# A linear-attention and FFN kernel: another planned order of the first tile, and batch 0's key sums from a product with a column of ones

## The chip, the cores and the metric

The kernel runs on one core of one Trainium2 chip. The metric is the device time of one execution in microseconds (us), the median of several. The engines are TensorE (PE; weight loads are a row of their own, PEld), VectorE (DVE), ScalarE (ACT) and GpSimd (POOL). SyncE (SP) only issues DMAs here.

## The reference

q, k and v have 8 batches, 8 heads, a sequence of 576 and a head size of 64. The attention is linear: no product of queries with keys, but a 64 by 64 matrix for each head.

```python
q_s = exp(q - max(q, axis=d));   q_s /= sum(q_s, axis=d) + 1e-9
k_s = exp(k - max(k, axis=seq)); k_s /= sum(k_s, axis=seq) + 1e-9
kv  = einsum('bhsd,bhse->bhde', k_s, v)
x   = einsum('bhsd,bhde->bhse', q_s, kv)      # -> 4608 tokens x 512
h   = maximum(x @ w_in, 0)                    # 512 -> 2048
out = (h * h) @ w_out                         # 2048 -> 512
```

The two weight matrices arrive in double precision; q, k and v in single.

## The kernel before

**Tiles.** The work is done in nine tiles of 512 tokens. Tiles 0 to 7 are the first 512 positions of each batch; the last 64 positions of all batches (their x goes to the DRAM tensor `x_tail`) make the ninth. A batch's eight heads are handled as four pairs p of two heads (128 channels). The hidden size is cut into 16 steps f of 128.

**The FFN of a tile.** For each f, the first product `h_f` is 12 matmuls of 512 columns: for each of the four pairs high half of x times high half of w_in, low half of x times high half, high half of x times low half (`xh`, `xl`; x is split into two rounded parts so that the sum is close to single precision). After relu and square, split again, the second product adds into four accumulators `acc_0` to `acc_3` (128 tokens each), three matmuls each.

**Weights.** The 16 "words" u (`load_words`, L478) are the weights as 64-bit numbers, 1 MB each in two halves of 512 KB: word 0 has the w_in blocks of f = 0 and 1, word u the w_in block of f = u + 1 and the w_out block of f = u − 1, the last two what is left. ACT scales both 32-bit parts of a word (`scale_words`: two rows `raw` of 1024), DVE and POOL join them (`join_words`), ACT casts the high half (row `w`) and POOL subtracts for the low half. Words 0 to 11 have their own buffers. Words 12 to 15 lie in a pool `late`, which can only be opened when every tile of the pool `boot` (batch 0's attention) has been used for the last time.

**Batch 0 ("boot").** The first tile needs batch 0's x, so this attention runs ahead of any FFN work. For each pair: k is transposed (`kT`, PE), DVE takes the maximum along the sequence, ACT does exp (`first_exp`, L826) with the sum along the row taken as the engine goes (`accum_out`, an extra ACCUMULATOR read), exp of the tail's 64 positions likewise, POOL adds both sums, DVE takes the reciprocal (`ks2`); PE transposes back (`ek`, `ekt`), `kv_product` (L905) multiplies with v (8 matmuls of 64 columns and 2 for the tail), `kv_split` (L949) scales by `ks2` on its way out of PSUM. `x_product` (L978) multiplies with the transposed q (`qT`) in two halves of 288 columns; ACT copies the high part, DVE subtracts for the low part, ACT copies the tail's 64 columns to `xt`. A single-precision matmul shows as two records.

**Batch 1 and later.** Batch 1's attention is interleaved with the FFN of tile 0. Its k stays untransposed: DVE reduces k, then a second step takes in the k tail (`kt`), a small step `sm` follows, PE transposes the maximum (`kmT`) and the rest follows; the denominators there come from a column of ones beside v, so that `ps[:, D]` of the kv product has the sum (`kv_scale`, L939, which for batch 0 returns at once).

**What sets the order.** Everything recorded for tile 0 (all such rows show line L100) goes through `Planner` (L126). Each instruction, or group under `together`, is a node with a cost; `order` (L256) walks through time, takes the earliest node that can start and, among those on its engine within `WAIT`, the one with the greatest priority (`tail`); a load ends at the running DMA time plus `moved / RATE` plus `LAND`. `shift` moves the priorities of some nodes for each number in `SEEDS`. The result is the program order of every engine, SP included. `fill` (L1511) puts transposes that nobody reads (`idle`, L1514) into PE's planned gaps before the first h. After tile 0's attention work everything has a fixed order.

Of the kernel before, what the change touches and what calls it, by code (L numbers as in the profile page):

```python
# [15 lines left out]
AF = mybir.ActivationFunctionType  # L16
ALU = mybir.AluOpType
# [97 lines left out]
class Node:  # L115


    def __init__(self, engine):
# [4 lines left out]
        self.since = 0.0  # L123


class Planner:  # L126
# [5 lines left out]
    ISSUE, LAND, RATE = 0.65, 2.2, 350.0  # L132
    READY, COLD, FILL, SPARE = 1.0, 0.25, 0.14, 0.2
    WAIT = 0.25

# [7 lines left out]
    def together(self, chained=False):  # L143
# [6 lines left out]
        node, self.into = self.into, None  # L150
        if chained:
            if self.chain is not None:
                node.before[self.chain] = True
            self.chain = node
# [101 lines left out]
    def order(self):  # L256
# [7 lines left out]
        free, dma, told = {}, 0.0, []  # L264
        self.banks = {}
        while ready:
# [20 lines left out]
            )  # L287
            n.start, n.end = t, t + n.busy
# [48 lines left out]
def attention_ffn(  # L337
# [26 lines left out]
    B, H, SQ, D = q.shape  # L364
    DM = H * D
    DF = w_in.shape[1]
    P = 128
# [13 lines left out]
    STEP = 0.0  # L381
    SEEDS = (
# [556 lines left out]
    def kv_scale(b, p):  # L939

        if b == 0:
            return
# [1256 lines left out]
```

## Time and profile before

| | |
|---|---|
| median of 3 runs | 829.72 us (829.48 to 831.48) |
| the profiled execution | 830.97 us |
| its span in the trace | 829.0 us |
| mean granted TensorE clock | 0.999 |

A profile row names an engine, a line, an operation and its tile with what it reads, then partitions by elements. Buffer numbers are left out in the trace's answers, so `h` is `h_f` of any step. "[0.81 <-ACT xh]" behind a row is the time that the engine stood idle ahead of it, and what released it. In the chain of waits each line is a start, a length and what the end of the program hung on there. For DMA issues the columns are count, size of each, and the time from issue to landing.

### The profile page before, as it was taken

Reading aid. Unit: us, or ns where it says so; the run is one execution under the profiler, and the core shown is the slowest. Engines: PE = TensorE matmul, PEld = TensorE weight load, DVE = VectorE, ACT = ScalarE, POOL = GpSimd, SP = SyncE. Lnnn points to the kernel's source line nnn. Section 1 sums busy time; section 2 is a strip of 40 time slices with the busy share of each in tenths; the row PEclk is TensorE's granted clock in tenths of the full one; section 3 lists DMA queues with packets and bytes.
Section 4 is the critical chain, followed back from the end, with each engine's and each line's share of the span. In section 5 each row is a group of like instructions: output and inputs, shape, how many; then the busy total and the mean of one; then the engine's idle time right before and its main releaser. Section 6 shows DMA issues by size and latency. Waiting matters only on the chain.

```text
span 829.0 us, 12870 instructions
## 1 busy us (share of the span) xinstructions
PE 816.2 (98%) x4411; PEld 662.5 (80%) x4411; DVE 620.5 (75%) x1134; ACT 481.7 (58%) x882; POOL 143.9 (17%) x151
## 2 busy tenths in 40 slices
PE   8999999999999999999999999999999999999997
PEld 7677777788888888788888787888888888888886
DVE  6888876877668656878667675577888987866995
ACT  6988844665655555655565566455754545665442
POOL 5889990001001001001001000000310000000000
PEclk9999999999999999999999999999999999999999
DMA  9993114435535446355446452766776778579455
GB/s 274 379 342 129 39 28 135 124 111 147 120 115 125 128 160 173 99 170 119 117 134 148 151 141 96 235 225 212 261 283 196 226 229 238 181 237 385 136 173 98
DMA packets 219297, 145.48 MB, mean 175 GB/s; under 512 B 146528, under 2 KB 193120, under 8 KB 219232
## 3 DMA queue, kind: packets, MB, share of 16 engines
q1 hardware_dynamic: 213312, 142.96, 56.9%
q10 hardware_dynamic: 5920, 1.71, 0.9%
q8 instruction: 35, 0.57, 0.3%
q14 instruction: 30, 0.25, 0.1%
HBM read 97.52 MB, written 46.66 MB: 174 GB/s over the span
## 4 chain that ended last, share of the span: by engine, by line
PE 84%; DMA 5%; SPq 4%; DVE 4%; ACT 2%; issue 1%; POOL 0%; DVEq 0%; ACTq 0%
PE acc L100 22%; PE h L100 20%; PE out L1865 18%; PE h L1308 17%; SPq L100 4%; PE h_kv L100 2%; PE x L100 2%; DMA k<-in_k_dram 1%; DMA qn<-in_k_dram 1%; DMA raw<-in_moe_w_out_dram 1%; DMA ring<-w_sums 1%; DVE bst L100 1%; ACT r L100 1%; DVE km L100 0%; DMA kt<-in_k_dram 0%
## 5 line engine op out<-in xcount | busy, mean ns | idle before, releaser
L100 PE MATMUL h<-xh,w 128*128 128x512 f32 x632 | 208.8, 392 | 1.0 <-ACT xh L100 0.8
L100 PE MATMUL acc<-w,gh 128*128 128x512 f32 x632 | 197.2, 393 | 0.0
L1865 PE MATMUL out<-w,w 128*128 128x512 f32 x636 | 148.9, 389 | 0.0
L100 PEld LDWEIGHTS h<-xh,w 128*128 128x128 f32 x632 | 118.6, 188 | 27.9 <-ACT xh L100 1.3
L1865 PEld LDWEIGHTS out<-w,w 128*128 128x128 f32 x636 | 119.3, 188 | 25.1 <-DVE w L100 0.2
L100 PEld LDWEIGHTS acc<-w,gh 128*128 128x128 f32 x632 | 117.0, 188 | 26.3 <-issue 1.7
L100 PE MATMUL acc<-w,gl 128*128 128x512 f32 x316 | 123.1, 390 | 0.0
L100 PE MATMUL h<-xl,w 128*128 128x512 f32 x316 | 123.1, 389 | 0.0
L100 DVE TENSOR_TENSOR gl<-r,gh 128x512 fp32r<-128x512 f32 x64 | 44.1, 688 | 73.2 <-ACT gh L100 72.6
L100 ACT ACTIVATE r<-h 128x512 f32<-128x512 f32 x79 | 47.1, 596 | 85.2 <-PE h L100 85.0
L100 POOL PARTITION_ALL_REDUCE kmx<-km x24 | 26.7, 1111 | 337.2 <-DVE km L100 337.2
L100 PEld LDWEIGHTS h<-xl,w 128*128 128x128 f32 x316 | 59.4, 188 | 12.5 <-DVE xl L100 0.4
L100 PEld LDWEIGHTS acc<-w,gl 128*128 128x128 f32 x316 | 59.3, 188 | 12.4
L1308 PE MATMUL h<-w,w 128*128 128x512 f32 x288 | 69.2, 389 | 0.0
L100 ACT COPY u<-h 128x512 f32<-128x512 f32 x48 | 28.0, 583 | 62.8 <-PE h L1308 62.7
L1308 PEld LDWEIGHTS h<-w,w 128*128 128x128 f32 x288 | 54.1, 188 | 11.2
L100 ACT CAST gh<-r 128x512 fp32r<-128x512 f32 x64 | 39.5, 617 | 21.5 <-PE acc L100 21.0
L100 ACT CAST w<-w 128x1024 fp32r<-128x1024 f32 (+1 forms) x38 | 38.0, 1006 | 18.4 <-PE out L1865 8.7
L1308 PE MATMUL h<-w,ring 128*128 128x512 f32 x192 | 46.4, 390 | 0.2 <-DMA ring<-w_sums 0.2
L100 DVE TENSOR_TENSOR c<-h,u 128x512 f32<-128x512 f32 x48 | 33.0, 687 | 13.6 <-ACT u L100 7.0
L1308 PEld LDWEIGHTS h<-w,ring 128*128 128x128 f32 x192 | 35.9, 188 | 8.1 <-PE h L1308 0.6
L100 POOL TENSOR_TENSOR w<-w,raw 128x512 int32<-128x512 int32 x32 | 41.8, 1327 | 1.7 <-DVE w L100 1.1
(236 smaller groups left out, 1290.1 us busy)
## 6 DMA issues: line engine op xcount, KB each, us to landing
w<-wo_sums SPq DMA_DIRECT2D x64, 256.0 KB, 3.4
g_b<-c SPq DMA_DIRECT2D x60, 256.0 KB, 2.6
w<-g_b SPq DMA_DIRECT2D x18, 512.0 KB, 7.8
raw<-in_moe_w_in_dram SPq DMA_DIRECT2D x16, 512.0 KB, 7.9
raw<-in_moe_w_out_dram SPq DMA_DIRECT2D x16, 512.0 KB, 8.5
v<-in_v_dram SPq DMA_DIRECT2D x56, 128.0 KB, 3.0
q<-in_q_dram SPq DMA_DIRECT2D x96, 72.0 KB, 2.3
k<-in_k_dram SPq DMA_DIRECT2D x20, 256.0 KB, 4.1
```

The lines of the kernel that those rows point to most:

```text
L100: getattr(self.eng, op)(*map(real, args), **{k: real(a) for k, a in kwargs.items()})
L1308: nc.tensor.matmul(out=out.real(), lhsT=a[:, k * P:(k + 1) * P].real(), rhs=m[k].real(), start=(begin and k == 0 and i == 0), stop=(k == 1 ...
L1865: nc.tensor.matmul(out=banks[name][m].real(), lhsT=a[:, m * P:(m + 1) * P].real(), rhs=b[:, i, :].real(), start=fresh and j == i == k == 0 ...
```

## The change

Three things are edited.

1. The planner's model. `RATE` goes from 350 to 360, the DMA time begins at `BEGIN` = 1.8, and the `kb` figure given with each load is no longer its size but a count by packets: 549 and 476 for the halves of a word in place of 512, 274 for 256, 157 for 72, 207 for 128, 104 for 64. When PE goes from FFN groups to others or back, `TURN` is added. The 108 numbers in `SEEDS` are replaced by 60 others. The planned order of all engines comes out anew.
2. Batch 0's sums. `first_exp` no longer sums; the two POOL adds and the reciprocal are gone. `kv_product` of batch 0 puts behind each 64-column matmul one with the `ones` tile (one column) into column D, and the tail's matmul takes v and its column of ones together, 65 columns. `kv_scale` then works as for the other batches: DVE adds 1e-9 to the column and takes the reciprocal.
3. x of batches 0 and 1. `x_product` computes 512 columns and 64 in place of 288 and 288; ACT copies the 512 in one instruction, DVE subtracts in one (batch 0); batch 1's x goes through ACT alone where DVE did 224 columns. The copy of the 64 columns is given a priority higher by `HURRY` = 60.

The core of the diff (the remaining `kb` figures are left out):

```diff
         self.before, self.after, self.soon = {}, {}, []
         self.buffers, self.behind = [], None
         self.start = self.end = self.tail = None
-        self.since = 0.0
+        self.since, self.large = 0.0, False
 
 
 class Planner:
...
 
 
     HOP = 0.12
-    ISSUE, LAND, RATE = 0.65, 2.2, 350.0
+    ISSUE, BEGIN, LAND, RATE = 0.65, 1.8, 2.2, 360.0
     READY, COLD, FILL, SPARE = 1.0, 0.25, 0.14, 0.2
     WAIT = 0.25
+    TURN = {True: 0.17, False: 0.08}
 
     def __init__(self):
         self.open, self.nodes, self.into, self.chain, self.boot = True, [], None, None, []
...
         self.into = "next"
         yield
         node, self.into = self.into, None
+        node.large = chained
         if chained:
             if self.chain is not None:
                 node.before[self.chain] = True
...
             for b in n.buffers:
                 b.placed = None
         ready = [n for n in self.nodes if not left[n]]
-        free, dma, told = {}, 0.0, []
+        free, dma, told = {}, self.BEGIN, []
+        large, matrix = None, self.marks[0].engine
         self.banks = {}
         while ready:
             able = []
...
                 ((t, n) for t, n in able if n.engine is n0.engine and t <= t0 + self.WAIT),
                 key=lambda x: x[1].tail,
             )
+            if n.engine is matrix:
+                if large not in (None, n.large):
+                    t += self.TURN[n.large]
+                large = n.large
             n.start, n.end = t, t + n.busy
             free[n.engine] = n.end
             if n.moved:
...
     LINE = 5
     SOON = 4
     STEP = 0.0
+    HURRY = 60.0
     SEEDS = (
-        95300002, 95300003, 95300006, 95300008, 95300016, 95300018, 95300030, 95300031,
...
+        700000, 700001, 700002, 700007, 700030, 700065, 700073, 700124, 700133,
...
     )
     EASE = 0.0
     EARLY = 2
...
             to = raw[:, h, :].only(f"{h}0", f"{h}1")
             if which == "i":
                 src = w_in[:, f * P:(f + 1) * P].rearrange("(kc p) f -> p kc f", p=P)
-                Y.dma_start(out=to.rearrange("p (a b) -> p a b", b=P), in_=src, kb=512)
+                Y.dma_start(out=to.rearrange("p (a b) -> p a b", b=P), in_=src, kb=549)
             else:
-                Y.dma_start(out=to, in_=w_out[f * P:(f + 1) * P, :], kb=512)
+                Y.dma_start(out=to, in_=w_out[f * P:(f + 1) * P, :], kb=476)
         raws.append(raw)
...
 
         kr = made.pop(("k", 0, p)).rearrange("p c h d -> p (c h d)")
         ps, kc = made.pop(("kT", p))
-        ks = small([P, 2], "ks2", f"ks2_{p}")
-        S.activation(out=kr, in_=ps, func=AF.Exp, bias=kc, accum_out=ks[:, 0:1], n=620)
+        S.activation(out=kr, in_=ps, func=AF.Exp, bias=kc)
         kt = made["kt", 0].rearrange("p h d -> p (h d)")
         at = (p % 2 * 2 + p // 2) * TL
         here = kt[:, at:at + TL].only(p)
-        S.activation(out=here, in_=here, func=AF.Exp, bias=kc, accum_out=ks[:, 1:2], n=150)
-        G.tensor_scalar_add(ks[:, 0:1], ks[:, 0:1], EPS, n=8)
-        G.tensor_tensor(out=ks[:, 0:1], in0=ks[:, 0:1], in1=ks[:, 1:2], op=ALU.add, n=8)
-        V.reciprocal(out=ks[:, 0:1], in_=ks[:, 0:1], n=8)
-        made["ks", p] = ks[:, 0:1]
+        S.activation(out=here, in_=here, func=AF.Exp, bias=kc, n=64)
         made["ekT", p] = kr
 
     def first_turn(p):
...
         kr, vr = made.pop(("ek", b, p)), made.pop(("v", b, p))
         tl, th = tail_of(b, p)
         ps = bank(f"kv_{b}_{p}", b == 0) if ps is None else ps
-        w = 2 * D if b == 0 else W
         if b == 0:
             ekt = made.pop(("ekt", p))
             parts = [(kr[:, c, :], None) for c in range(C)]
...
             at = p * (W + 1)
             parts = [(kr[:, c, :], vr[:, c, :]) for c in range(C)] + [(ekt, v_tail[:, at:at + W])]
 
-        n = D if b == 0 else D + 1
+        n = D + 1
         with plan.together():
             for i, (k_part, v_part) in enumerate(parts):
                 for j in range(2):
                     rows, cols = slice(j * D, (j + 1) * D), slice(j * D, j * D + n)
+                    if b == 0:
+                        at = slice(j * n, j * n + D)
+                        T.matmul(
+                            out=ps[rows, at], lhsT=k_part[:, rows], rhs=vr[:, j, i, :],
+                            start=(i == 0), stop=False, n=2 * D,
+                        )
+                        T.matmul(
+                            out=ps[rows, D:n], lhsT=k_part[:, rows], rhs=ones[:, 0:1],
+                            start=False, stop=False, n=60,
+                        )
+                        continue
                     T.matmul(
                         out=ps[rows, cols], lhsT=k_part[:, rows],
-                        rhs=vr[:, j, i, :] if b == 0 else v_part[:, cols],
-                        start=(i == 0), stop=(b > 0 and i == C), n=2 * n,
+                        rhs=v_part[:, cols],
+                        start=(i == 0), stop=(i == C), n=2 * n,
                     )
             if b == 0:
                 for j in range(2):
-                    rows = slice(j * D, (j + 1) * D)
+                    rows, cols = slice(j * D, (j + 1) * D), slice(j * D, j * D + n)
                     T.matmul(
-                        out=ps[rows, rows], lhsT=ekt[:, rows],
-                        rhs=v_heads[tl, 2 * p + j, 0:D].only(p // 2),
+                        out=ps[rows, cols], lhsT=ekt[:, rows],
+                        rhs=v_tail[tl, p * (W + 1):p * (W + 1) + W][:, cols].only(p // 2),
                         start=False, stop=True, n=2 * n,
                     )
         made["kvp", b, p] = ps
 
     def kv_scale(b, p):
 
-        if b == 0:
-            return
         ps = made["kvp", b, p]
         ks = small([P, 1], "ks", f"ks_{b}_{p}")
         V.tensor_scalar_add(ks, ps[:, D:D + 1], EPS, n=8)
...
     def kv_split(b, p):
 
         ps, ks = made.pop(("kvp", b, p)), made.pop(("ks", p))
-        at_of = D if b == 0 else D + 1
+        at_of = D + 1
         kv = kv_parts[(b * NP + p) % 2]
         for j in range(2):
             at = slice(j * D, (j + 1) * D)
...
 
         kv, turned = made.pop(("kv", b, p)), made.pop(("qT", b, p))
         heads = [slice(j * D, (j + 1) * D) for j in range(2)]
-        for i in range(2):
-            cs = slice(i * SH, (i + 1) * SH)
-            ps = bank(f"x_{b}_{p}_{i}", b == 0)
+        main, tail = (bank(f"x_{b}_{p}_{i}", b == 0) for i in range(2))
+        for ps, cs in ((main, slice(0, M)), (tail, slice(M, SQ))):
+            n = cs.stop - cs.start
             with plan.together():
                 for rows in heads:
                     T.matmul(
-                        out=ps[rows, 0:SH], lhsT=kv[:, rows], rhs=turned[:, cs], start=True,
-                        stop=True, n=2 * SH,
+                        out=ps[rows, 0:n], lhsT=kv[:, rows], rhs=turned[:, cs], start=True,
+                        stop=True, n=2 * n,
                     )
-            n = min(cs.stop, M) - cs.start
-            xs = slice(cs.start, cs.start + n)
-            if b == 0:
-                hi, lo = (part[:, xs].only(i) for part in x[p])
-                S.copy(out=hi, in_=ps[:, 0:n], n=n)
-                V.tensor_tensor(out=lo, in0=ps[:, 0:n], in1=hi, op=ALU.subtract, n=n)
-            elif i:
-                V.tensor_copy(out=x[:, p, xs].only((p, i)), in_=ps[:, 0:n], n=n)
-            else:
-                S.copy(out=x[:, p, xs].only((p, i)), in_=ps[:, 0:n], n=n)
-            if i:
-                if p == 0:
-                    made["xt", b] = small([P, NP, TL], "xt", f"xt_{b}", 1)
-                xt = made["xt", b]
-                S.copy(out=xt[:, p, :].only(p), in_=ps[:, n:SH], n=TL)
+        if b == 0:
+            hi, lo = x[p]
+            S.copy(out=hi, in_=main)
+            V.tensor_tensor(out=lo, in0=main, in1=hi, op=ALU.subtract)
+        else:
+            S.copy(out=x[:, p, :], in_=main)
+        if p == 0:
+            made["xt", b] = small([P, NP, TL], "xt", f"xt_{b}", 1)
+        xt = made["xt", b]
+        eased, plan.ease = plan.ease, -HURRY
+        S.copy(out=xt[:, p, :].only(p), in_=tail[:, 0:TL], n=TL)
+        plan.ease = eased
         if p == NP - 1:
-            Y.dma_start(out=x_tail[:, :, b * TL:(b + 1) * TL], in_=xt, kb=128)
+            Y.dma_start(out=x_tail[:, :, b * TL:(b + 1) * TL], in_=xt, kb=207)
 
     def x_two(b, p, x, spare=None):
```

**Where the order moves: ACT.** ACT's queue around the scaling of word 1 (`raw_1`), before. `kv0` and `kv1` are the outputs of `kv_split`, `w0` is word 0's cast, `x_0_p` batch 0's products.

```order
L100 ACTIVATE kv1_95<-kv_0_1_423,ks2_1_320 64x64
L100 COPY ek_0_2_459<-ek_2_444 128x512
L100 ACTIVATE kv1_95<-kv_0_1_423,ks2_1_320 64x64
L100 CAST xh_0_0_484<-x_0_0_0_439 128x288
L100 ACTIVATE raw_1_252<-raw_1_252 128x1024
L100 COPY xt_0_506<-x_0_1_1_489 128x64
L100 CAST xh_0_1_508<-x_0_1_1_489 128x224
L100 ACTIVATE kv0_93<-kv_0_2_473,ks2_2_434 64x64 x2
L100 CAST xh_0_1_508<-x_0_1_0_498 128x288
L100 CAST xh_0_0_484<-x_0_0_1_503 128x224
L100 COPY xt_0_506<-x_0_0_1_503 128x64
L100 CAST w0_543<-w_0_467 128x2x512
```

After:

```order
L100 ACTIVATE raw_1_262<-raw_1_262 128x1024
L100 ACTIVATE kv1_95<-kv_0_1_445,ks_0_1_479 64x64 x2
L100 CAST w0_514<-w_0_411 128x2x512
L100 ACTIVATE k_0_3_229<-kT_3_406,kc_0_3_464 128x512
L100 ACTIVATE raw_1_262<-raw_1_262 128x1024
L100 ACTIVATE kv0_93<-kv_0_2_495,ks_0_2_524 64x64 x2
L100 CAST xh_0_0_565<-x_0_0_0_482 128x512
L100 ACTIVATE kt_0_167<-kt_0_167,kc_0_3_464 128x64
L100 CAST xh_0_1_578<-x_0_1_0_521 128x512
L100 COPY ek_0_3_583<-ek_3_559 128x512
```

The first scaling of `raw_1` now stands ahead of pair 1's split, word 0's cast and pair 2's split; both scalings stand ahead of every `xh`.

**SP.** The loads around batch 1's first k (`k_1_0`, tails `kt_1`), before:

```order
L100 DMA raw_10_546<-in_moe_w_in_dram 128x4x128
L100 DMA q_1_0_555<-in_q_dram 128x2x256
L100 DMA raw_10_546<-in_moe_w_out_dram 128x512
L100 DMA raw_11_573<-in_moe_w_in_dram 128x4x128
L100 DMA raw_11_573<-in_moe_w_out_dram 128x512
L100 DMA k_1_0_611<-in_k_dram 128x2x256
L100 DMA kt_1_618<-in_k_dram 64x4x64 x2
L100 DMA v_tail_158<-in_v_dram 64x4x64
L100 DMA v_1_1_656<-in_v_dram 128x4x64 x2
L100 DMA raw_12_679<-in_moe_w_in_dram 128x4x128
```

After:

```order
L100 DMA raw_10_519<-in_moe_w_in_dram 128x4x128
L100 DMA v_1_0_526<-in_v_dram 128x4x64 x2
L100 DMA raw_10_519<-in_moe_w_out_dram 128x512
L100 DMA raw_11_554<-in_moe_w_in_dram 128x4x128
L100 DMA k_1_0_567<-in_k_dram 128x2x256
L100 DMA q_1_0_576<-in_q_dram 128x2x256
L100 DMA raw_11_554<-in_moe_w_out_dram 128x512
L100 DMA kt_1_597<-in_k_dram 64x4x64 x2
L100 DMA v_tail_158<-in_v_dram 64x4x64
L100 DMA v_1_1_644<-in_v_dram 128x4x64 x2
```

`k_1_0` has moved ahead of q of the same pair and of the w_out half of word 11; `kt_1` still stands behind the same loads. Before, words 12 to 15 follow directly; after, they follow the loads of pair 1 and of pair 2's q and k.

**PE.** Around the first h product (`h_0`), before:

```order
L100 MATMUL x_0_2_1_548<-qT_0_2_517,kv0_93 64x288 x2
L100 MATMUL qT_0_3_557<-ident_86,qn_0_3_538 128x128 x4
L1514 MATMUL idle_162<-ident_86 128x128 x6
L100 MATMUL h_0_0_583<-xh_0_0_484,w0_543 128x512
L100 MATMUL h_0_0_583<-xl_0_0_492,w0_543 128x512
L100 MATMUL h_0_0_583<-xh_0_0_484,w0_543 128x512
L100 MATMUL h_0_0_583<-xh_0_1_508,w0_543 128x512
L100 MATMUL h_0_0_583<-xl_0_1_523,w0_543 128x512
L100 MATMUL h_0_0_583<-xh_0_1_508,w0_543 128x512
L100 MATMUL ek_3_599<-ident_86,k_0_3_235 128x128 x4
L100 MATMUL ekt_3_609<-ident_86,kt_0_167 128x128
L100 MATMUL h_0_0_583<-xh_0_2_562,w0_543 128x512
```

After:

```order
L100 MATMUL ek_3_559<-ident_86,k_0_3_229 128x128 x4
L100 MATMUL x_0_2_0_569<-qT_0_2_548,kv0_93 64x512 x2
L1514 MATMUL idle_162<-ident_86 128x128 x3
L100 MATMUL ekt_3_591<-ident_86,kt_0_167 128x128
L100 MATMUL h_0_0_593<-xh_0_0_565,w0_514 128x512
L100 MATMUL h_0_0_593<-xl_0_0_580,w0_514 128x512
L100 MATMUL h_0_0_593<-xh_0_0_565,w0_514 128x512
L100 MATMUL kv_0_3_606<-v_0_3_250,ek_0_3_583 64x64
L100 MATMUL kv_0_3_606<-ones_91,ek_0_3_583 64x1
L100 MATMUL kv_0_3_606<-v_0_3_250,ek_0_3_583 64x64
L100 MATMUL kv_0_3_606<-ones_91,ek_0_3_583 64x1
```

Pair 3's transposes now stand ahead of the first h and its qT behind; x is one product of 512 columns; between the matmuls of `kv_0_3` stand those with `ones`. Further on, batch 1's first `kmT` stands behind four accumulators of the third step instead of three, its second `kmT` in a step before, and the tail of batch 0's last x in step 7. From the end of tile 0's attention on, the order of every engine is that of before.

More of the change, by code (lines that the diff above doesn't have):

```diff
@@ L558, in load_kq @@
         to = "p c h d" if turned else "p h c d"
-        queue.dma_start(out=t, in_=src.rearrange(f"h (p c) d -> {to}", c=C), kb=256)
+        queue.dma_start(out=t, in_=src.rearrange(f"h (p c) d -> {to}", c=C), kb=274)
         made[which, b, p] = t
@@ L570, in load_q_blocks @@
                     in_=q[b, 2 * p + j, :, a * Q:(a + 1) * Q].rearrange("(g t) d -> t g d", t=Q),
-                    kb=72,
+                    kb=157,
                 )
@@ L586, in load_v @@
                 out=t, in_=v[b, 2 * p:2 * p + 2, 0:M, :].rearrange("h (p c) d -> p h c d", c=C),
-                kb=256,
+                kb=274,
             )
@@ L596, in load_v @@
                 in_=v[b, 2 * p + j, 0:M, :].rearrange("(p c) d -> p c d", c=C),
-                kb=128,
+                kb=207,
             )
@@ L610, in load_tail_kq @@
                 in_=src[b, g * GH:(g + 1) * GH, M:SQ, :].rearrange("h p d -> p h d"),
-                kb=64,
+                kb=104,
             )
@@ L619, in load_tail_v @@
                 in_=v[b, g * GH:(g + 1) * GH, M:SQ, :].rearrange("h p d -> p h d"),
-                kb=64,
+                kb=104,
             )
@@ L1044, in x_two @@
         if p == NP - 1:
-            Y.dma_start(out=x_tail[:, :, b * TL:(b + 1) * TL], in_=xt, kb=128)
+            Y.dma_start(out=x_tail[:, :, b * TL:(b + 1) * TL], in_=xt, kb=207)
     def x_tiles(t):
```

20 rows, old and new, of the table SEEDS are left out of this document.

## The prediction

> **What bounds the kernel now.** I read the profile's totals first, then busy time by stages of the first tile, then TensorE's timeline to place the gaps, then the chain of waits across them, and last ACT's queue ahead of the first product.
>
> ```profile
> span 829.0 us, 12870 instructions
> PE 816.2 (98%) x4411; PEld 662.5 (80%) x4411; DVE 620.5 (75%) x1134; ACT 481.7 (58%) x882; POOL 143.9 (17%) x151
> ```
>
> TensorE is busy 98% of the span, so the whole kernel holds 12.8 us in which it is not. The windows say where. Columns: busy us of PE, weight loads, DVE, ACT and POOL, granted clock, DMA share, GB/s.
>
> ```profile
> 0.00:27.60 27.60, 23.56 (x205) 18.51 (x205) 20.05 (x51) 18.36 (x44) 16.05 (x34) 1.00 0.99 300
> 27.60:56.13 28.53, 25.84 (x135) 19.83 (x134) 23.66 (x44) 24.12 (x38) 24.92 (x26) 1.00 1.07 361
> 56.13:135.02 78.89, 78.86 (x428) 60.37 (x427) 64.81 (x116) 56.70 (x88) 64.04 (x60) 1.00 0.30 88
> 135.02:829.00 693.98, 687.94 (x3649) 563.78 (x3647) 511.93 (x926) 382.55 (x714) 38.94 (x33) 1.00 0.58 173
> ```
>
> From 56.13 us to the second tile at 135.02 TensorE idles 0.03 us of 78.89. Behind that the instruction order of every engine is the same in both kernels. So all the change can win or lose is TensorE's work in the first tile, the idle time ahead of 56.13 us, and idle time that it makes afterwards. Part of "busy" before 27.60 us is filler transposes (L1514), so the start of the first h product is the better mark there. TensorE's timeline around it and around the two gaps (the bracket is idle time ahead of a row, and its releaser):
>
> ```profile
> 27.02 0.82 PE L1514 MATMUL idle<-ident 128*128 128x128 f32 x6
> 27.60 0.48 PE L100 MATMUL h<-xh,w 128*128 128x512 f32 x1
> 35.57 0.50 PE L100 MATMUL h<-xh,w 128*128 128x512 f32 x1 [0.81 <-ACT xh L100]
> 40.12 0.61 PE L100 MATMUL acc<-w,gh 128*128 128x512 f32 x2
> 55.29 0.30 PE L100 MATMUL kmT<-ident,km 128*128 128x128 f32 x1 [1.84 <-DVE sm L100]
> 56.13 0.39 PE L100 MATMUL h<-xh,w 128*128 128x512 f32 x1
> ```
>
> Two waits, 0.81 us (for the high half of x of pair 3) and 1.84 us (for the key maximum of batch 1's first pair). The chain of waits names their feeders, and the load that held ACT ahead of the first product (15.76):
>
> ```profile
> 15.76 6.73 DMA raw<-in_moe_w_out_dram
> ...
> 29.23 0.44 PE ek L100 x4
> 29.67 0.11 PE ekt L100
> 31.17 0.90 PE kv L100 x20
> 43.69 9.55 DMA k<-in_k_dram
> 53.26 1.07 DVE km L100
> 54.35 0.79 DVE km L100
> ```
>
> The load of batch 1's k took 9.55 us behind everything queued ahead of it; DVE's two maximum steps follow, then TensorE may go on. So before 56 us the kernel is bound by transfers: the DMA share is 0.99 and 1.07.
>
> **First h product: +1.4 us.** ACT's rows up to it:
>
> ```profile
> 22.57 1.17 ACT L100 ACTIVATE raw<-raw 128x1024 f32<-128x1024 f32 x1 [0.83 <-DMA raw<-in_moe_w_out_dram]
> 23.63 0.18 ACT L100 COPY xt<-x 128x64 f32<-128x64 f32 x1
> 23.96 0.64 ACT L100 ACTIVATE kv<-kv,ks 64x64 f32<-64x64 f32 x2
> 24.62 0.65 ACT L100 CAST xh<-x 128x288 fp32r<-128x288 f32 x2
> 25.41 1.05 ACT L100 CAST w<-w 128x1024 fp32r<-128x1024 f32 x1
> 26.37 0.39 ACT L100 CAST xh<-x 128x288 fp32r<-128x288 f32 x1
> 28.06 0.70 ACT L100 ACTIVATE k<-kT,kc 128x512 f32<-128x512 f32 x1
> 28.62 0.22 ACT L100 ACTIVATION_READ_ACCUMULATOR k<-kT,kc 128x1 f32 x1
> ```
>
> Word 1's first scaling starts at 22.57 because its load lands then. SP's order up to that load is untouched, and the transfers share the same full engines, so it lands at the same time after the change. What moved is ACT: that scaling now stands ahead of pair 1's kv split, word 0's cast, pair 3's exp, a second scaling, and pair 2's split. From start to next start the rows give 1.06 for a scaling (22.57 to 23.63), 0.66 for a split (23.96 to 24.62), 0.96 for a cast (25.41 to 26.37), 0.56 for an exp (28.06 to 28.62). From 22.57: 23.63, 24.29, 25.25, 25.81, 26.87, 27.53. Then TensorE does pair 2's x. A record of 288 columns is 0.14 by starts (26.53 less 25.41, by eight):
>
> ```profile
> 25.41 1.19 PE L100 MATMUL x<-qT,kv 128*64 128x288 f32 x8
> 26.53 0.66 PE L100 MATMUL qT<-ident,qn 128*128 128x128 f32 x4
> 31.10 0.69 PE L100 MATMUL kv<-v,ek 128*64 128x64 f32 x16
> 31.72 0.33 PE L100 MATMUL kv<-v_tail,ekt 64*64 64x64 f32 x4
> 31.98 0.50 PE L100 MATMUL h<-xh,w 128*128 128x512 f32 x1
> ```
>
> A record of 512 columns is then 0.14 × 512/288 = 0.249, and a matmul is two records, so the pair's two matmuls take 1.0: 28.53. Three fillers at 0.097 (27.02 to 27.60, by six) 0.29, pair 3's tail transpose 0.11: the first h starts at about 28.95, against 27.60: +1.35, say +1.4. The DVE edits of batch 0 (a sum and reciprocal from PSUM in place of POOL's two adds and a reciprocal) and the dropped accumulator reads (28.62's row) lie under this queue and count nothing; without the cover they are tenths of a microsecond.
>
> **Boot work behind the first h: +0.7 us.** Before, pair 3's transposes, kv and x stand there: 0.44 + 0.11 + 0.90 + 1.12 = 2.57. The qT are four transposes like ek's. After, kv (0.90), its new ones products, two x tails, qT (0.44) and pair 3's x (1.0). No row shows a matmul with a one-column moving side. The nearest is the kv record of 64 columns, 31.10 to 31.72 by 16 = 0.039; from below I bound it by taking a third of that, 0.014, since its moving side is a 64th but its load is not smaller. Sixteen records are 0.22 to 0.62; I take 0.62, as the loads are equal. Two tails are eight 64-column records, 0.31 (by the tail row, 31.72 to 31.98 by four, 0.52). Sum 0.90 + 0.62 + 0.31 + 0.44 + 1.0 = 3.27: +0.7.
>
> The Trainium skill, page "TensorE: Matmul & The Clock Gate", section "LDWEIGHTS (loading the stationary operand)", puts a weight load at its columns divided by 1.2 in nanoseconds, 53 ns for 64 columns, which would be 0.85 us for these sixteen if loads set the pace, and 0.2 us more in the sum. This case's trace speaks against that as a floor: the kv records with their own loads come every 39 ns.
>
> **The 0.81 us wait: gone.** It stood ahead of pair 3's high half of x. Before, 36 h products stand between the first h and the first acc, 40.12 − 27.60 − 0.81 − 2.57 = 9.14 us of them, 0.25 each. After, nine h products, kv, a tail, qT and pair 3's x end at 28.95 + 2.3 + 1.52 + 0.15 + 0.44 + 1.0 = 35.4; ACT's copy of 512 columns is as long as the exp (0.56), DVE's subtraction taken as long: due at 36.5. TensorE has nine more products and a tail first, to 37.8. −0.81. What is late next is batch 1's k.
>
> **The 1.84 us wait: gone.** In SP's new order k of batch 1's first pair is issued ahead of one w_out half and of q, which both stood before it; the k tails still stand behind the same set of loads. The issues and their landings, median us:
>
> ```profile
> k<-in_k_dram SPq DMA_DIRECT2D x1, 256.0 KB, 9.6
> kt<-in_k_dram SPq DMA_DIRECT2D x2, 64.0 KB, 8.5
> 44.43 1.82 SPq L100 DMA_DIRECT2D kt<-in_k_dram  x2
> ```
>
> One half-word and one q are 0.77 MB less ahead of k; at about 0.39 MB per us (the 361 GB/s of the second window, a little more at its fullest) 2.0 us: k lands at 43.69 + 9.55 − 2.0 = 51.2. The tails land where they did, about 45 + 8.5 = 53.5. DVE's reduce of k (1.07) is over before they land, and only the second step (0.79) and sm (0.14, to 55.29) are behind: ready at about 54.6. TensorE's own arrival: 28.95 + 9.14 + 3.27 = 41.36 at the first acc. From there to the wait 55.29 − 1.84 − 40.12 = 13.33, and one acc more, as kmT now stands behind four (0.73: 55.29 to 56.13 less a transpose's 0.11): 55.4. So no wait, by 0.8 us: −1.84. If this cover is gone, each us by which the tails land later than 54.3 is a us of wait.
>
> **Later.** Pair 3's x tail of batch 0 stands in a later step, four records, +0.15. Batch 1's four x pairs go from 1.12 to 1.0 + 0.15 each, +0.1. ACT's copy of 512 in place of ACT 288 and DVE 224 lies under TensorE.
>
> Sum: 1.4 + 0.7 − 0.81 − 1.84 + 0.15 + 0.1 = −0.3. The profiled execution took 830.97 us about its span of 829.0 (1.9 around it); it becomes 830.67. The median is 829.72, 1.25 below the profiled time, so 829.4 is the forecast. What this kernel's measurement can tell from no change is about 0.3%, 2.5 us, so the bounds are 827.2 and 832.2.
>
> **Rivals.** Faster: the loads land sooner. ACT would be free for word 1's scaling near 20.4, and its 2.1 us of waiting go if the load has landed by then; the k tails must land as much sooner, or the 0.8 us of cover turns into a wait. With the ones products at their lower price (0.4 less) the sum is −0.3 − 2.1 − 0.4 = −2.8: 826.9. For it: each wait in the first 56 us ends on a transfer. Against: same issues, DMA share 0.99.
>
> Slower: the late words. Loads of words 12 to 15 were issued here, beginning at 50.31:
>
> ```profile
> 50.31 1.59 SPq L100 DMA_DIRECT2D raw<-in_moe_w_in_dram  x1
> 79.56 2.79 PE acc L100 x11
> 100.92 3.90 POOL L100 TENSOR_TENSOR w<-w,raw 128x512 int32<-128x512 int32 x3
> 104.74 2.56 POOL L100 TENSOR_TENSOR w<-w,w 128x512 fp32r<-128x512 f32 x2
> 107.95 0.40 PE L100 MATMUL h<-xh,w 128*128 128x512 f32 x1
> ```
>
> Their pool opens when the boot's last tile is done with, now pair 3's x tail, which stands in an acc of step 7 (79.56 on): so issues start at about 83, behind k and q of pair 2. A word is 1 MB, 2.8 us at 361 GB/s, and with batch 1's v and latency it lands near 89; two ACT scalings and DVE's join make 93.6. POOL joined word 12 at 100.92 and split it up to 107.3, and h of step 13 began at 107.95. In the new POOL order, words 12 and 13 are joined (four at 1.30) and three and more splits at 1.28 stand up to word 12's last, some 10.8 us with the small ones: it must start by about 96.9. That leaves 3.3 us. If the words are 6.8 us later than I have them, TensorE waits 3.5 us: 832.9. For it: 33 us later issue. Against: after 56 us DMA share is only 0.30.
>
> Small new waits: batch 1's second kmT stands one step earlier, and its maximum is due within 0.5 us of TensorE's arrival; with the ones products at 0.85 and one such wait +1.0: 830.4. Nothing for or against it but the thin margin.
>
> That the change does nothing: it is the forecast's sign that is small, not its terms; not a case of its own.
>
> The section "Wait — 56ns, not 53.3ns?" of that page of the Trainium skill has a fixed cost per matmul of about 2.5 ns; no run here shows it for a one-column product.
>
> **How the numbers follow.** Forecast 0.61, faster rival 0.12, small waits 0.16, late words 0.11. The likeliest is 829.4. The forecast's own range, ones products from 0.22 to 0.85 and the two gaps each right within half a microsecond, is 828.4 to 830.4. To hold eight in ten the range reaches to the small waits and towards both ends: 827.0 to 831.6. Faster by over 0.3% takes the first rival, 0.12; slower takes the late words, 0.11; the rest 0.77.
>
> **What the profile after would show.** Right: word 1's scaling at 22.57 on ACT with a longer idle ahead of it; the first h at about 29.0; kv of pair 3 with its ones products 1.5 us long; no gap ahead of pair 3's x_h; kmT with no idle before it at about 55.4; late loads issued near 83 and no gap at step 13; the second tile at 134.7 against 135.02. Wrong: a first h before 28, word 1's load landing at another time, a new gap over 0.5 us between 56 and 135, or any difference behind the second tile's start, where the orders agree.

## The result, and the profile after

The changed kernel took 837.24 us (median of 4 runs, 836.82 to 838.0) against 830.6 us before (4 runs, 829.48 to 831.75): ratio 1.0081, 95% interval 1.0062 to 1.0100. It is slower, by 6.6 us, and outside the forecast range. The span of its profiled execution is 835.8 us against 829.0, granted clock 0.999 in both.

TensorE's timeline of the changed kernel, at the places that the prediction named (start, length, operation, idle time ahead and its releaser in brackets):

```profile
28.95 0.48 PE L100 MATMUL h<-xh,w 128*128 128x512 f32 x1
41.21 0.62 PE L100 MATMUL acc<-w,gh 128*128 128x512 f32 x2
55.95 0.30 PE L100 MATMUL kmT<-ident,km 128*128 128x128 f32 x1 [0.71 <-ACT raw L100]
67.39 0.33 PE L100 MATMUL kmT<-ident,km 128*128 128x128 f32 x1 [0.50 <-DVE km L100]
136.01 0.40 PE L100 MATMUL h<-xh,w 128*128 128x512 f32 x1
472.74 0.69 PE L100 MATMUL h_kv<-v,ek 128*64 128x65 f32 x16 [2.08 <-ACT xt L100]
```

The same place as the last of these, before:

```profile
468.87 0.69 PE L100 MATMUL h_kv<-v,ek 128*64 128x65 f32 x16 [0.50 <-ACT xt L100]
```

The second tile starts at 136.01 us against 135.02. So the first tile, the only place where the order differs, has at most +1.0 us of the 6.8 by which the span grew (its last steps use the late words too). The rest arises where the order of every engine is that of before: 1.58 us in one wait (2.08 less 0.50), and the other 4.2 us outside the waits. One run of products of the last stage shows where, 49 records one behind another, with the row that follows. Before:

```profile
598.15 11.27 PE L1865 MATMUL out<-w,w 128*128 128x512 f32 x49
609.26 0.39 PE L1865 MATMUL out<-w 128*128 128x512 f32 x1
```

After:

```profile
602.49 11.47 PE L1865 MATMUL out<-w,w 128*128 128x512 f32 x49
613.80 0.40 PE L1865 MATMUL out<-w 128*128 128x512 f32 x1
```

From start to next row, 11.11 us by 49 is 226.7 ns a product; after the change 11.31 by 49 is 230.8 ns. The same instructions on the same shapes, with no idle time, take 1.8% longer. The second products of the tiles pay as well, here as a group from 141 us on, before and then after (count, busy us, mean ns):

```profile
L100 PE MATMUL acc<-w,gh 128*128 128x512 f32 x512 | 159.1, 392 | 0.0
```

```profile
L100 PE MATMUL acc<-w,gh 128*128 128x512 f32 x512 | 160.1, 394 | 0.0
```

Over the same stretch the products of L1865 grew from 148.9 to 150.8 us, those of acc with gl from 99.7 to 100.1, and those of L1308 with `w` on both sides from 69.2 to 69.8, each with an equal count before and after. Together these four groups have 3.9 of the 4.2 us.

What differs there is not in the order but in the addresses. SBUF is the memory on the chip from which TensorE reads; an address here is a byte within each of its 128 partitions. The change drops the two small tiles `ks2`, which took 32 bytes of a partition each. What lies behind them in SBUF, batch 0's tiles and then words 12 to 15 in the same space, moved down by 64 bytes: word 12 starts at byte 196288 in the built program, where it started at 196352, a multiple of 256, before. Other tiles changed places too, as tiles are placed in the order in which the planned program first uses them; the large ones ahead of the small tiles moved by multiples of 256 bytes. The first theory was therefore: a product is slower when TensorE reads words 12 to 15 at the new place. Its rival: the new order of the first tile, or the exchanged places of other tiles, is behind the loss.

### The profile page after: what moved, and what is told of

Its sections match the earlier page's. It is cut to its first block, busy times and chain, and to the rows that moved or that the text cites. A ratio compares the mean times of both kernels' runs of the same rounds, so it can differ in the third digit from the quotient of the medians.

```text
span 835.8 us, 12976 instructions
## 1 busy us (share of the span) xinstructions
PE 822.5 (98%) x4473; PEld 663.9 (79%) x4473; DVE 620.0 (74%) x1130; ACT 482.4 (58%) x870; POOL 142.8 (17%) x143
## 4 chain that ended last, share of the span: by engine, by line
PE 87%; DMA 4%; DVE 3%; ACT 3%; issue 1%; SPq 1%; POOL 0%; ACTq 0%; DVEq 0%; POOLq 0%
PE acc L100 23%; PE h L100 20%; PE out L1865 18%; PE h L1308 18%; PE h_kv L100 2%; PE x L100 2%; DMA qt<-in_q_dram 1%; DMA qn<-in_k_dram 1%; SPq L100 1%; PE kv L100 1%; DMA v<-in_v_dram 1%; ACT raw L100 1%; DVE bst L100 1%; DVE km L100 1%; DMA q<-in_q_dram 1%
## 5 line engine op out<-in xcount | busy, mean ns | idle before, releaser
L1865 PE MATMUL out<-w,w 128*128 128x512 f32 x636 | 150.8, 392 | 0.0
L1865 PEld LDWEIGHTS out<-w,w 128*128 128x128 f32 x636 | 119.3, 188 | 27.0
L1308 PE MATMUL h<-w,w 128*128 128x512 f32 x288 | 69.8, 391 | 0.0
L1308 PEld LDWEIGHTS h<-w,w 128*128 128x128 f32 x288 | 54.1, 188 | 11.8
L1308 PE MATMUL h<-w,ring 128*128 128x512 f32 x192 | 46.3, 390 | 0.0
L100 POOL TENSOR_TENSOR w<-w,w 128x512 fp32r<-128x512 f32 x32 | 41.3, 1302 | 7.2 <-ACT w L100 6.9
```

Source lines behind the costliest of these rows:

```text
L100: getattr(self.eng, op)(*map(real, args), **{k: real(a) for k, a in kwargs.items()})
L1308: nc.tensor.matmul(out=out.real(), lhsT=a[:, k * P:(k + 1) * P].real(), rhs=m[k].real(), start=(begin and k == 0 and i == 0), stop=(k == 1 ...
L1865: nc.tensor.matmul(out=banks[name][m].real(), lhsT=a[:, m * P:(m + 1) * P].real(), rhs=b[:, i, :].real(), start=fresh and j == i == k == 0 ...
```

## The experiments

All ratios are against the kernel before on the same chip. The first four kernels move the late words alone.

**The late words back up by 64 bytes**, in the changed kernel:

```diff
-        late.pool.tile([P, 16], F32, tag="pad3", name="pad3")
+        late.pool.tile([P, 32], F32, tag="pad3", name="pad3")
```

> The changed kernel with the pad ahead of the late words 64 bytes larger, so that words 12 to 15 lie at byte 196352 of a partition as before (after the change: 196288). The order of every engine is that of the changed kernel. Theory address (words 12 to 15 off a 128-byte line slow TensorE's reads of them by some 6 ns a product): the matmul spacing behind the second tile's start returns to about 227 ns, some 4 us of the 6.6 lost come back: ratio to before about 1.003, 833.1. Theory order (the loss comes from the new order of tile 0 or the other tiles' places that moved with it): no difference to the changed kernel, ratio 1.008, 837.

Measured 832.01 us, ratio 1.0010 (0.9997 to 1.0024). A pad that nobody reads gives back 1.0081 − 1.0010, nearly all of the loss.

**The late words down by 64 bytes**, in the kernel before (the pad left out):

```diff
-        late.pool.tile([P, 16], F32, tag="pad3", name="pad3")
+        pass
```

> The kernel before with the pad ahead of the late words left out, so that words 12 to 15 lie at byte 196288 as after the change; nothing else moves. Theory address: about 4 us slower than before, ratio 1.005, with acc products at some 232 ns where they read late words. Theory order: no difference, ratio 1.000.

Measured 835.61 us, ratio 1.0052 (1.0033 to 1.0071): most of the loss, without the change.

**The late words up by 32 and by 128 bytes**, in the kernel before (`[P, 24]` and `[P, 48]` in the same line):

> The kernel before with the pad 32 bytes larger: words 12 to 15 at 196384, 32 bytes off a 64-byte line. Theory address, if any offset within a 128-byte line costs: slower by about 4 us, ratio 1.005; if a 64-byte piece is what is read at once, at least as much and perhaps twice, 1.01. Theory order: 1.000.

> The kernel before with the pad 128 bytes larger: words 12 to 15 at 196480, on a 128-byte line but off a 256-byte line. Theory address with a 128-byte line: no difference, 1.000. If the line is 256 bytes, or the place itself matters: slower, up to 1.005. Theory order: 1.000.

Measured 837.79 us, ratio 1.0079 (1.0061 to 1.0096), and 836.2 us, ratio 1.0062 (1.0043 to 1.0081). Words 12 to 15 on a 128-byte line are not enough. The same 49 products in the kernel with the late words back up, and in the three others (down 64, up 32, up 128):

```profile
599.07 11.27 PE L1865 MATMUL out<-w,w 128*128 128x512 f32 x49
```

```profile
601.75 11.47 PE L1865 MATMUL out<-w,w 128*128 128x512 f32 x49
```

```profile
601.41 11.56 PE L1865 MATMUL out<-w,w 128*128 128x512 f32 x49
```

```profile
599.58 11.50 PE L1865 MATMUL out<-w,w 128*128 128x512 f32 x49
```

The rival is out for this part of the loss: three of these kernels lose without the change. But "each read off its line costs" was not yet told apart from "the late words lie badly to the others".

**Every tile up by 128 bytes**, in the kernel before:

```diff
-    const.pool.tile([P, 32], F32, tag="pad", name="pad")
+    const.pool.tile([P, 64], F32, tag="pad", name="pad")
```

> The kernel before with the first pad of SBUF 128 bytes larger, so that every tile, words 0 to 15, x, g and the late words alike, lies 128 bytes higher; no order changes and no tile moves against another. Theory line (a TensorE read costs more when its own start is off a 256-byte line): every product pays what only the late words' paid when they alone were moved by 128, the spacing goes from 227 to 231 ns and more over the whole program: 12 to 16 us slower, ratio 1.014 to 1.02. Theory neighbours (it is the place of late words against other tiles or their split over some boundary that counts): no difference or a small one, 1.000 to 1.002.

Measured 835.95 us, ratio 1.0057 (1.0038 to 1.0076). Neither theory gave this. The trace separates two things. The 49 products are as fast as before, so it is not each operand's own line that counts. And the loss lies in the first tile: the second tile starts at 140.25 us against 135.02. There the DMAs moved 10% less in the same 30 us (this kernel, then before; last column GB/s), and TensorE got the first key maximum 4 us later.

```profile
602.54 11.27 PE L1865 MATMUL out<-w,w 128*128 128x512 f32 x49
...
15.00:45.00 30.00, 27.20 (x218) 19.90 (x217) 24.95 (x51) 25.85 (x52) 24.57 (x32) 1.00 1.06 329
...
59.28 0.30 PE L100 MATMUL kmT<-ident,km 128*128 128x128 f32 x1 [3.75 <-DVE sm L100]
```

```profile
15.00:45.00 30.00, 28.44 (x223) 20.98 (x222) 26.22 (x55) 27.36 (x53) 25.07 (x33) 1.00 1.06 367
```

**The late words and batch 0's tiles down by 256 bytes**, in the kernel before (`pad2` of 44 in place of 108):

> The kernel before with the pad in the small tiles' pool 256 bytes smaller: words 12 to 15 at 196096, another 256-byte line, batch 0's tiles 256 bytes lower too. Theory line with 256 bytes: no difference, 1.000. Theory of this one place (or of a 512-byte line: 196352 lies 256 off one, 196096 on one): a change of up to 0.6% either way.

Measured 830.82 us, ratio 0.9996 (0.9977 to 1.0015): no difference, which fits a distance that counts modulo 256.

**The products by themselves**, in a program of its own. `mov` and `wgt` are the bytes by which the moving operand and the weights lie off a 256-byte line; N is 96, M 512, P 128:

```python
    for name, mov, wgt in GROUPS:
        ...
        for n in range(N):
            at = (n % 4) * M + mov // 4
            wt = 8 * M + (n % 8) * P + wgt // 4
            nc.tensor.matmul(
                out=ps, lhsT=big[:, wt:wt + P], rhs=big[:, at:at + M], start=(n == 0), stop=(n == N - 1)
            )
```

> None of the reference's work: 17 groups of 96 products of 128x512 with 128x128 weights, from one tile of zeros that lies on a 256-byte line; in a group the moving operand, or the weights, or both start 0, 8, 32, 64, 128, 192 or 256 bytes off the line; the output is zeros. Theory line, moving side: spacing 227 ns at 0 and 256, 231 to 236 at the others for the moving operand, and 227 for all weights groups. Theory line, both sides: weights off the line cost some 2 to 6 ns too. Theory neighbours or contention with other engines' accesses: 227 in all groups, as nothing else runs.

From its timeline (one run); the second column is the length of a group. "mov" moves the moving operand, "wgt" the weights, "both" the two of them, "full" is by 256 bytes, "none" by nothing:

```profile
55.52 22.56 PE L44 MATMUL mov_thirtytwo<-big 128*128 128x512 f32 x96
77.92 22.14 PE L44 MATMUL mov_sixtyfour<-big 128*128 128x512 f32 x96
99.89 22.46 PE L44 MATMUL mov_onetwentyeight<-big 128*128 128x512 f32 x96
122.19 22.57 PE L44 MATMUL mov_oneninetytwo<-big 128*128 128x512 f32 x96
144.60 21.96 PE L44 MATMUL mov_full<-big 128*128 128x512 f32 x96
166.40 21.92 PE L44 MATMUL none_b<-big 128*128 128x512 f32 x96
232.72 22.56 PE L44 MATMUL wgt_sixtyfour<-big 128*128 128x512 f32 x96
255.11 22.46 PE L44 MATMUL wgt_onetwentyeight<-big 128*128 128x512 f32 x96
277.42 22.15 PE L44 MATMUL wgt_oneninetytwo<-big 128*128 128x512 f32 x96
321.18 21.96 PE L44 MATMUL both_sixtyfour<-big 128*128 128x512 f32 x96
342.98 21.97 PE L44 MATMUL both_onetwentyeight<-big 128*128 128x512 f32 x96
```

Against 21.92 us, either operand off by 32 to 192 bytes costs 0.2 to 0.65 us per 96 products, 2 to 7 ns each; both off by the same amount cost 0.05 us at most. It is the distance between weights and moving operand, modulo 256 bytes, and even its direction: the moving operand 64 up and the weights 192 up are the same distance and take 22.14 and 22.15, the other way round 22.57 and 22.56. No other engine is needed for it; in this program ACT only copies each group's result out.

The probe gives the size in the kernel as well, as an estimate. Of the 3264 FFN products in the built programs, 928 take a late word, 448 as weights and 480 as moving operand. Late words down by 64 lie 192 off, modulo 256; by the lengths of the probe's groups that adds 2.4 ns where the weights are moved and 6.8 ns where the moving operand is, 4.3 us in all. In the same way, late words up by 32 make 6.2 us (weights up by 32 took 22.56 too) and up by 128 5.2 us. The ratios measured for these three kernels are worth 4.3, 6.6 and 5.2 us, with intervals of about 1.6 us either way.

**Batch 0's tiles back as well**, in the changed kernel (`pad2` of 124 in place of 108):

> The changed kernel with the pad in the small tiles' pool 64 bytes larger, as if the two small tiles that the change drops were still there: batch 0's tiles and words 12 to 15 both lie where they lay before. Theory address of the late words alone: as the changed kernel with the late words up 64, 832.0, ratio 1.001. If the place of batch 0's tiles counts as well: a further 0.1% or more either way.

Measured 832.54 us, ratio 1.0019 (0.9999 to 1.0038): as with the late words alone. The place of batch 0's tiles adds nothing that shows.

**Two DVE steps moved**, on top of that. In the planned order, the step that takes the tail into the key maximum goes ahead of the reduce of q:

```diff
+        for p in range(2):
+            km, mx = f"km_1_{p}", f"mx_1_{p}"
+            names = {n: {b.name for b in n.buffers} for n in told}
+            vector = [n for n in told if km in names[n] and "kt_1" in names[n]]
+            other = [n for n in told if mx in names[n] and n.engine is vector[0].engine]
...
+            vector[0].start = min(vector[0].start, other[0].start - 1e-6)
```

> The changed kernel with its small tiles' pool 64 bytes larger, and two of DVE's instructions moved: for batch 1's pairs 0 and 1 the step that takes the k tail into the key maximum now stands right behind the reduce of k, ahead of the reduce of q (and, for pair 0, of a word's join). Nothing else moves. Theory DVE queue (the waits of 0.75 and 0.45 us ahead of the two kmT are DVE's, not the tails' load): both waits go or shrink to under 0.2, some 1 us less than the same kernel without the move: 831.5 against 832.5. Theory tail load (the wait is for the k tails' landing): the wait for pair 0 stays at 0.6 to 0.8.

Measured 831.04 us, ratio 1.0004 (0.9995 to 1.0013). DVE's queue of the changed kernel, then of this one:

```profile
52.87 1.09 DVE L100 TENSOR_REDUCE km<-k 128x128 f32<-128x512 f32 x1
53.88 0.68 DVE L100 TENSOR_REDUCE mx<-q 128x8 f32<-128x512 f32 x1
54.47 0.69 DVE L100 SCALAR_TENSOR_TENSOR w<-raw,up 128x512 int32<-128x512 int32 x1
55.06 0.74 DVE L100 TENSOR_TENSOR km<-km,kt 64x128 f32<-64x128 f32 x1
```

```profile
52.30 1.09 DVE L100 TENSOR_REDUCE km<-k 128x128 f32<-128x512 f32 x1
53.52 0.46 DVE L100 TENSOR_TENSOR km<-km,kt 64x128 f32<-64x128 f32 x1
```

And TensorE's first kmT in this one, with no idle time ahead:

```profile
54.47 0.27 PE L100 MATMUL kmT<-ident,km 128*128 128x128 f32 x1
```

Both kmT waits are gone, so they were DVE's queue and not the tails' load. The whole is level with the kernel before. The difference to the run without the move lies within the intervals, and no version here is faster than the kernel before.

**Loads by themselves**, for the first tile's loss when all tiles moved by 128:

```python
            for n in range(N):
                at = n * M + off // 8
                to = big[:, at:at + M]
                if kind == "o":
                    nc.sync.dma_start(out=to, in_=w_out[n * P:(n + 1) * P, :])
                ...
```

The elements have 64 bits, `off` is in bytes, N is 6 and M 512; w_in blocks are loaded in the same way.

> None of the reference's work: six loads at a time of w_out blocks, then of w_in blocks (512 KB each), into a tile whose pieces start 0, 32, 64, 128 or 256 bytes off a 512-byte line, and 0 again; the output is zeros. Theory load place (the first tile's 5 us when all tiles lay 128 bytes higher come from slower writes into SBUF): the groups at 128 take 5 to 10% longer than those at 0 and 256; at 32 and 64 as much or more. Theory other cause: all groups within 2%.

DVE reads a column of each load as it lands; the second and the last of six, for w_in blocks at 0, at 128 and at 256 bytes:

```profile
91.75 0.15 DVE L40 COPY seen_i_none<-i_none 128x1 int32<-128x1 int32 x1 [1.11 <-DMA i_none<-in_moe_w_in_dram]
...
97.17 0.15 DVE L40 COPY seen_i_none<-i_none 128x1 int32<-128x1 int32 x1 [1.16 <-DMA i_none<-in_moe_w_in_dram]
...
126.62 0.15 DVE L40 COPY seen_i_onetwentyeight<-i_onetwentyeight 128x1 int32<-128x1 int32 x1 [1.31 <-DMA i_onetwentyeight<-in_moe_w_in_dram]
...
132.57 0.15 DVE L40 COPY seen_i_onetwentyeight<-i_onetwentyeight 128x1 int32<-128x1 int32 x1 [1.27 <-DMA i_onetwentyeight<-in_moe_w_in_dram]
...
138.25 0.15 DVE L40 COPY seen_i_twofiftysix<-i_twofiftysix 128x1 int32<-128x1 int32 x1 [1.21 <-DMA i_twofiftysix<-in_moe_w_in_dram]
...
143.66 0.15 DVE L40 COPY seen_i_twofiftysix<-i_twofiftysix 128x1 int32<-128x1 int32 x1 [1.16 <-DMA i_twofiftysix<-in_moe_w_in_dram]
```

By four, a load of 512 KB in pieces of 1 KB lands every 1.36, 1.49 and 1.35 us: 10% slower 128 bytes off, which fits the 10% that the DMAs of the first tile lost when all tiles moved. For the w_out blocks the landings are too uneven in this one run to tell a few per cent.

**Everything up by 192 but the late words, batch 0's tiles and the small ones**, in the changed kernel, which makes the distance a multiple of 256 again with neither operand on a line (first pad of 80 in place of 32, `pad2` of 60 in place of 108):

> The changed kernel with words 12 to 15 and batch 0's tiles where the change put them, and every other tile 192 bytes higher, so that weights and moving operands are again a multiple of 256 bytes apart although none lies on a 256-byte line. Theory apart (it is the distance between the two operands that counts): the spacing behind the second tile's start returns to 227 ns, 4 us less there; the first tile loses some 5 us as it did when all tiles were moved by 128: 836 to 839 in all. Theory line (each operand's own start counts): the spacing rises to 231 ns and more in all products, 12 us more than the changed kernel: 849.

Measured 836.27 us, ratio 1.0066 (1.0046 to 1.0086), and the 49 products:

```profile
603.40 11.27 PE L1865 MATMUL out<-w,w 128*128 128x512 f32 x49
```

The theory of the distance holds in the kernel itself. The first tile pays, as expected: the second tile starts at 139.19 us, against 136.01 in the changed kernel.

## Why the prediction was wrong, point by point

**The step that failed** is the first: "Behind that the instruction order of every engine is the same in both kernels. So all the change can win or lose is TensorE's work in the first tile, the idle time ahead of 56.13 us, and idle time that it makes afterwards." The orders are indeed the same; the time is not. Two tiles of 32 bytes that went with `ks2` put words 12 to 15 at another distance to the tiles that they are multiplied with, and every product that reads a late word beside another tile takes a few ns more, 4.2 us behind the second tile's start in the profiled executions. None of the rivals had it, though "any difference behind the second tile's start" stood among the things that would prove the prediction wrong. The kernel before already had pads in the small pool and ahead of the late words, and what they are for was not asked.

**First h product, +1.4: right.** It starts at 28.95, the figure worked out. ACT's queue is the predicted one, from word 1's scaling at its load's landing to pair 2's split. The load landed as before (22.38 against 22.57), so the faster rival did not come:

```profile
22.38 1.17 ACT L100 ACTIVATE raw<-raw 128x1024 f32<-128x1024 f32 x1 [1.93 <-DMA raw<-in_moe_w_out_dram]
23.45 0.62 ACT L100 ACTIVATE kv<-kv,ks 64x64 f32<-64x64 f32 x2
...
25.75 1.15 ACT L100 ACTIVATE raw<-raw 128x1024 int32<-128x1024 uint32 x1
26.80 0.62 ACT L100 ACTIVATE kv<-kv,ks 64x64 f32<-64x64 f32 x2
```

**Boot work, +0.7: near, by luck, as two wrong sizes cancel.** Pair 3's kv with its ones products, first and last rows:

```profile
29.83 0.34 PE L100 MATMUL kv<-v,ek 128*64 128x64 f32 x4
30.00 0.24 PE L100 MATMUL kv<-ones,ek 128*64 128x1 f32 x4
...
30.88 0.33 PE L100 MATMUL kv<-v_tail,ekt 64*64 64x65 f32 x4
31.14 0.34 PE L100 MATMUL x<-qT,kv 128*64 128x64 f32 x4
31.41 0.66 PE L100 MATMUL qT<-ident,qn 128*128 128x128 f32 x4
```

From 29.83 to 30.88, less 0.62 for the 64-column records, sixteen ones products take 0.43 us, 27 ns each, between the bounds and below the 39 taken; the x tail takes 0.27 (31.14 to 31.41), where 0.15 was taken and the other row had said 0.26. The Trainium skill ("TensorE: Matmul & The Clock Gate", "LDWEIGHTS (loading the stationary operand)") would make it 53 ns for each, an estimate from its rule of columns divided by 1.2: the trace shows half of that. The first acc came at 41.21, against 41.36.

**The 0.81 us wait: gone**, as forecast. One sum on the way there is wrong, since its terms from 28.95 on add up to 34.4 and not 35.4; both sides of the comparison hang on it, so the cover stays at 1.3 us. **The 1.84 us wait: not gone** but 0.71. TensorE arrived at 55.24 (forecast 55.4); the maximum was ready at 55.8, not 54.6. The working gave DVE the second step as soon as the tails had landed, and never looked at DVE's new queue, where two other steps stand ahead of it. The bracket of that row names ACT's scaling, but the DVE step ended at 55.80, and with that step moved ahead the wait was gone. The second kmT waited 0.50 us for the same cause; the rival of small waits had that one.

**Later terms: too small.** Batch 1's x pairs carry such tails of 0.27 as well, which makes about +0.6 in place of +0.1. With the two waits, +1.2, that is more than the 1.3 us between the second tile's start as forecast (134.7) and as measured (136.01); the first acc came 0.15 early, and the rest was not followed up.

**Late words: the rival did not come.** Their first load was issued at 85.87, near the 83 forecast, and POOL's joins began at 98.08; TensorE shows no idle time in step 13:

```profile
85.87 0.37 SPq L100 DMA_DIRECT2D raw<-in_moe_w_in_dram  x1
98.08 5.10 POOL L100 TENSOR_TENSOR w<-w,raw 128x512 int32<-128x512 int32 x4
```

So the order and the sums, which the prediction weighed, are worth 1.0010 and 1.0019 in the two runs with the late words put back, +0.8 and +1.6 us, both intervals touching no change; the forecast was −0.3 us.

**Open:** the 1.58 us at 472.74. The load of k that it hangs on took longer in the changed kernel. From the chains of waits, after and then before:

```profile
455.15 8.93 DMA qn<-in_k_dram
```

```profile
452.47 7.71 DMA qn<-in_k_dram
```

The wait was 1.0 to 1.6 us in the four other runs with the new order, and 0.5 or less in the six with the old one. So it goes with the change and not with the place of the late words. Other tiles of that stage did change places; why the load takes longer was not settled. Nor was why the distance between two operands counts. And most tiles of batch 0's q, k and v lie 192 bytes off a 256-byte line in the kernel before, 128 in the changed one; no run put them on one.

## What to carry to other kernels

Equal orders are not equal kernels: when an edit adds or drops a tile, compare the addresses in the built program before arguing that a stage cannot change. Keep the tiles that TensorE takes as weights and as moving operand a multiple of 256 bytes apart, and the places that loads write on 256-byte lines; a pad that nobody reads can do both. And a wait that a new order should remove has to be followed through the queue of every engine on its chain, not only through the transfers.

## What the runs showed of the hardware

A 128x512 product behind another takes 227 ns when weights and moving operand start a multiple of 256 bytes apart in a partition and 229 to 233 ns on average at the distances measured in between, in a program where other engines only copy out and store results. The Trainium skill ("TensorE: Matmul & The Clock Gate", "Part 2: What happens when you issue a matmul") has the next weights loading while the present product runs, without taking read bandwidth of SBUF from it. The probe differs: a product's time hangs on the distance between weights and moving operand, by 2 to 7 ns.

Loads of 1 KB pieces into places 128 bytes off a 256-byte line took 1.49 in place of 1.35 us for 512 KB. The Trainium skill ("DMA: Bandwidth & Descriptors", "How a descriptor splits into AXI transactions") lets a transaction start only on a 256-byte line, and bytes ahead of the start cost beats though they are not used. The page says this of what is read; carried over to the place written, as an estimate, such a piece costs 36 beats in place of 32, 12% more, and the measured 10% is near that. At 32 bytes off the same estimate gives 33 beats, 3% more, while the probe shows 1.49 us there too, so the rule does not account for what was measured.
